# Attention and two MLPs on one core: the softmax quotient and a share of the squares go from VectorE to ScalarE

## The chip, the cores and the metric

One Trainium2 chip, one of its cores. The metric is device time in microseconds (us), the median of several runs. The engines of the core work side by side, each through its own list of instructions in order: TensorE (PE in the rows, PEld its weight loads), VectorE (DVE), ScalarE (ACT), GpSimd (POOL) and SyncE (SP), whose queue here issues every DMA. TensorE writes into PSUM, in banks; GpSimd works on SBUF only.

## What is computed

The reference has three parts, in fp32. Attention over 2 batches, 8 heads, 768 tokens of 64 dimensions, with a mask from hash buckets:

```python
mask = q_bucket[:, :, :, None] == k_bucket[:, :, None, :]
scores = np.where(mask, scale * np.matmul(q, k.transpose(0, 1, 3, 2)), -1000000000.0)
attn = np.exp(scores - np.max(scores, axis=-1, keepdims=True))
attn = attn / (np.sum(attn, axis=-1, keepdims=True) + 1e-09)
x = np.matmul(attn, v)                       # then heads side by side: 1536 tokens x 512
```

Then two MLPs one after the other, 512 to 2048 to 512, each with weights of its own:

```python
r = np.maximum(x @ w_in, 0.0);  x = (r * r) @ w_out      # layer 0
h = x @ w_in;  out = np.maximum(0.01 * h, h) @ w_out     # layer 1
```

The inputs q, k, v, proj and the weights of both layers are float32 or wider, and the weights are unpacked on the chip from pairs of 32-bit words.

## The kernel before

**Slots.** Attention runs over 48 slots a batch: 4 pairs of heads, 2 heads, 6 tiles of 128 queries. A slot is: TensorE's scores (line 659, four matmuls), VectorE's row maximum (lines 679 and 683), ScalarE's exponential (line 688), and the transposition of the result p as two fp16 halves. The high half is a cast (lines 717 and 718), the low half a subtraction, on GpSimd (line 721) or VectorE (line 722). In batch 0 half of the slots go through TensorE for the transposition (lines 699, 707, 710), all others through a DMA (line 735). After that TensorE multiplies p with v (lines 756 to 758, 18 matmuls a slot, written into the PSUM tile `av`). `av` has two halves of three slots each. When three slots are summed, `finish` works out the quotient: on VectorE, `rd` = sum times scale (line 780), its reciprocal (line 784) and the product with the 3 x 64 columns (line 785) into `xtok`. A half of `av` can be written again after that.

Every 12 slots a new pair of heads is prepared (`prep`): sizes (line 441), scales over the partitions (`level`, lines 398 to 419), fp16 halves (lines 479, 492, 501), hash bits (lines 546, 558, 564), v (lines 608, 614).

**Banks for scores.** Batch 0 has three banks for scores, `s` and the two of `sx`. When the MLP begins, `sx` becomes the four banks `acc` of the MLP, so that batch 1 has the one bank `s`: the scores of a slot can be written when the maximum of the slot ahead has been read.

**MLP.** The weights of layer 0 are fetched, unpacked on VectorE (lines 883, 887, 890), split into a high part (lines 927, 928) and a low one (line 932), and written back for a second use. A unit of TensorE is 12 matmuls (lines 938 to 940). After an "up" unit of layer 0, ScalarE takes the Relu (line 977, `rt`), VectorE multiplies by it (line 980, `gx`), and the result is split again (lines 990 and 995). After a "down" unit the result is copied or added (lines 1059 and 1061). Four groups of 8 up and 8 down units make one batch of a layer.

**The stages.** Batch 0's attention comes first. Its results are transposed (line 802) and split (lines 811 and 812). Then layer 0 of batch 0 runs on TensorE between the slots of batch 1's attention. From 400 us on there is MLP alone: layer 0 of batch 1, then layer 1 of both.

**What sets the order.** Every step is given to `Plan` by `do(due, reads, writes, engine=(cost, function))`, with what it reads and writes, a due time, and a cost of its own for each engine that may do it; the first engine named is the one it prefers. `order` plays the steps through with these costs and places each on an engine at a time; the instructions are then written in that order, and stay in it on the chip. The constants at the head of the function (`DONE_AT`, `PITCH1` and the rest) shift due times.

Of the kernel before, what the change touches and what calls it, by code (L numbers as in the profile page):

```python
# [14 lines left out]
ACTF = mybir.ActivationFunctionType  # L15
ALU = mybir.AluOpType
# [158 lines left out]
def lsh_attention_moe_moe_kernel(  # L175
# [17 lines left out]
    nc = tc.nc  # L193
    B, H, S, D = q.shape
# [22 lines left out]
    SINGLE = 5  # L217
    BEHIND = 4
    BY_PE = 2
    PE_LAG = 3.65  # L220
    SECOND = -1.46
    VLATE = -5.42
    OWN = 0.30
    MARGIN = 0.99
    MAX_AT = 2.01
    EXP_AT = -0.44
    HI_AT = 7.80
    LO_AT = -14.89
    TURN_AT = -1.33
    DONE_AT = -8.87  # L230
    PREP_AT = -1.03
    PREP_STEP = 0.35
    LAG0 = -6.35
    FETCH = 13.02
    CONVERT = 16.38
    KEEP = -12.32
    AGAIN = 45.39
    FETCH0 = 3.26
    LEAD0 = 57.48
    CONVERT0 = -9.27  # L240
    LOAD1_AT = -14.58
    HALVE = 19.67
    T_UP = 16384.0
    SIZE16 = 6.00
    const = ctx.enter_context(tc.tile_pool(name="const", bufs=1))
# [518 lines left out]
    def finished(b, i, d):  # L764

        pr, n = divmod(i, SLOTS)
        h = n // NTB
        _, x3 = held[b, pr]
        half, x = i // HB % 2, i % HB
        summed.add((b, i))  # L770
        first = i - x
        if any((b, y) not in summed for y in range(first, first + HB)):
            return False
        tq = first % NTB + HB - 1
        rd = rd_[half]
        hh = 2 * pr + h

        def finish():
            acc = psum["av"][0][:, half]
            nc.vector.tensor_scalar(  # L780
                out=rd, in0=acc[:, :, D:D + 1], scalar1=SUM_EPS, scalar2=sc[x3][:, 2:3],
                op0=ALU.add, op1=ALU.mult,
            )
            nc.vector.reciprocal(out=rd, in_=rd)
            nc.vector.tensor_tensor(
                out=xtok[:, tq - HB + 1:tq + 1, hh * D:(hh + 1) * D], in0=acc[:, :, 0:D],
                in1=rd.to_broadcast([128, HB, D]), op=ALU.mult,
            )

        do(  # L790
            d + DONE_AT, [("av", half, y) for y in range(HB)] + [("sc", x3)], [("x", hh, tq // HB), ("rd", half)],
            dve=(0.75, finish),
        )
        return True

# [161 lines left out]
    def up(b, L, f, j, d):  # L957

        r = f % FG
        key, extra, bank = acc_bank()  # L960
        def part(c):
            w = w16(r) if L else (wi[:, r, 0, :], wi[:, r, 1, :])
            xs = [(x16(b, j, s) if L else xt[b, j, s])[:, c, :] for s in "hl"]
            three(bank()[:, :HALF], [y[:, c * 128:(c + 1) * 128] for y in w], xs, c == 0, c == NC - 1)

        us = (G1_T, G1_T16)[L]
        for c in range(NC):
            do(
                d, [("w16", r, y) if L else ("w", "i", r, y) for y in range(2)]
                + [("x16" if L else "xt", b, j, y, c) for y in "hl"],  # L970
                [key] + (extra if c == 0 else []), pe=(us / NC, lambda c=c: part(c)),
            )
        rt, gx = rt_[ring("rt", 2)], gx_[ring("gx", 2)]
        rk, gk = ("rt", turns["rt"] % 2), ("gx", turns["gx"] % 2)
        d += G1_T
        if L == 0:
            do(d, [key], [rk], act=(0.37, lambda: nc.scalar.activation(
                out=rt, in_=bank()[:, :HALF], func=ACTF.Relu
            )))
            do(d + 0.4, [key, rk], [gk], dve=(0.47, lambda: nc.vector.scalar_tensor_tensor(  # L980
                out=gx, in0=bank()[:, :HALF], scalar=0.0, in1=rt, op0=ALU.max, op1=ALU.mult
            )))
        else:
            do(d, [key, ("back", b)], [rk], act=(0.37, lambda: nc.scalar.activation(  # L984
                out=rt, in_=bank()[:, :HALF], func=ACTF.Copy, scale=back[b][:, 0:1]
            )))
            do(d + 0.4, [key, rk, ("back", b)], [gk], dve=(0.47, lambda: nc.vector.scalar_tensor_tensor(  # L987
                out=gx, in0=bank()[:, :HALF], scalar=back[b][:, 1:2], in1=rt, op0=ALU.mult, op1=ALU.max
            )))
        do(d + 1.1, [gk, "given"], [("g", r, j, 0)], act=(0.42, lambda: nc.scalar.copy(out=g_of(r, j)[0], in_=gx)),  # L990
           dve=(Port(0.27), lambda: nc.vector.tensor_copy(out=g_of(r, j)[0], in_=gx)))

        def low(eng):
            gh, gl = g_of(r, j)
            eng.tensor_tensor(out=gl, in0=gx, in1=gh.bitcast(FP32), op=ALU.subtract)  # L995

        do(d + 1.6, [gk] + [("g", r, j, 0)], [("g", r, j, 1)],
           pool=(0.98, lambda: low(nc.gpsimd)), dve=(Port(0.47), lambda: low(nc.vector)))
# [108 lines left out]
        return d  # L1107


    PITCH = 1.88  # L1110
    LEAD = 8.07
    START = 11.59
    MLP_OFF = 10.91
# [155 lines left out]
```

## Time and profile before

| | |
|---|---|
| median of 3 runs | 803.62 us (801.91 to 806.05) |
| the profiled execution, its own time | 803.74 us |
| its span, first to last instruction | 802.0 us |
| TensorE busy | 721.7 us (90%) |
| VectorE busy | 578.0 us (72%) |
| ScalarE busy | 433.3 us (54%) |
| GpSimd busy | 325.5 us (41%) |
| mean granted TensorE clock | 0.957 |
| chain of work that ended last | PE 75%, DVE 19%, issue 3%, ACT 2%, DMA 1% |

A busy share over the whole span mixes three stages with different limits. The table of busy time by stretch splits them: a stretch in which TensorE is busy throughout at a granted clock of 1.00 can be shortened only by giving it less to do, and in the others the question is what TensorE waits for. "Granted clock" is TensorE's clock as a share of 2.4 GHz; its lower level is 1.2 GHz.

### The profile page before, as it was taken

Reading aid. Unit: us, or ns where it says so; the run is one execution under the profiler, and the core shown is the slowest. Engines: PE = TensorE matmul, PEld = TensorE weight load, DVE = VectorE, ACT = ScalarE, POOL = GpSimd, SP = SyncE. Lnnn points to the kernel's source line nnn. Section 1 sums busy time; section 2 is a strip of 40 time slices with the busy share of each in tenths; the row PEclk is TensorE's granted clock in tenths of the full one; section 3 lists DMA queues with packets and bytes.
Section 4 is the critical chain, followed back from the end, with each engine's and each line's share of the span. In section 5 each row is a group of like instructions: output and inputs, shape, how many; then the busy total and the mean of one; then the engine's idle time right before and its main releaser. Section 6 shows DMA issues by size and latency. Waiting matters only on the chain.

```text
span 802.0 us, 14410 instructions
## 1 busy us (share of the span) xinstructions
PE 721.7 (90%) x5526; PEld 591.9 (74%) x5526; DVE 578.0 (72%) x1170; ACT 433.3 (54%) x739; POOL 325.5 (41%) x258
## 2 busy tenths in 40 slices
PE   3686767689999796899999999999999999999998
PEld 2474545477998684798899999996776766767766
DVE  6899999968998999989655544768547539638422
ACT  5877787647757577457555513456454044153330
POOL 2324233325565456558643614327025033232320
PEclk9899989869999997799999999999999999999999
DMA  3496777697998999998731324123303302210112
GB/s 118 78 219 108 189 149 207 120 236 139 222 264 165 185 248 227 197 270 179 163 77 50 94 64 132 30 76 105 105 1 106 105 1 87 81 44 27 40 40 78
DMA packets 185860, 100.81 MB, mean 126 GB/s; under 512 B 149440, under 2 KB 171968, under 8 KB 185792
## 3 DMA queue, kind: packets, MB, share of 16 engines
q1 hardware_dynamic: 185792, 99.90, 51.9%
q8 instruction: 43, 0.70, 0.4%
q14 instruction: 25, 0.20, 0.1%
HBM read 51.38 MB, written 11.53 MB: 78 GB/s over the span
## 4 chain that ended last, share of the span: by engine, by line
PE 75%; DVE 19%; issue 3%; ACT 2%; DMA 1%; POOL 0%; SPq 0%; DVEq 0%; ACTq 0%; POOLq 0%
PE acc L938 21%; PE acc L939 21%; PE acc L940 21%; PE s L659 4%; DVE ep L679 3%; PE av L756 2%; PE av L758 2%; PE av L757 1%; DVE s L492 1%; PE sx L699 1%; DVE lo L679 1%; DVE sm L683 1%; DVE pt L679 1%; DVE lg L679 1%; PE sx L659 1%
## 5 line engine op out<-in xcount | busy, mean ns | idle before, releaser
L995 POOL TENSOR_TENSOR g<-gx,g 128x384 fp32r<-128x384 f32 x113 | 124.5, 1115 | 164.6 <-ACT g L990 150.4
L721 POOL TENSOR_TENSOR ep<-ep 128x768 f16<-128x768 f32 x44 | 77.9, 1777 | 79.2 <-ACT ep L717 50.6
L932 POOL TENSOR_TENSOR wo<-w,wo 128x512 fp32r<-128x512 f32 x37 | 53.5, 1457 | 121.9 <-ACT wo L927 78.5
L938 PE MATMUL acc<-xh,wi 128*128 128x384 f32 x256 | 91.4, 357 | 1.2 <-DVE gx L980 1.0
L938 PE MATMUL acc<-g,wo 128*128 128x384 f32 x256 | 88.9, 347 | 1.8 <-DVE part L1061 1.3
L939 PE MATMUL acc<-xl,wi 128*128 128x384 f32 x256 | 87.7, 343 | 0.0
L940 PE MATMUL acc<-xh,wi 128*128 128x384 f32 x256 | 87.7, 343 | 0.0
L688 ACT ACTIVATE ep<-ep,sm,scs 128x768 f32<-128x768 f32 x60 | 61.6, 1027 | 47.5 <-DVE sm L683 46.2
L984 ACT ACTIVATE rt<-acc,rawq 128x384 f32<-128x384 f32 x64 | 37.1, 579 | 91.4 <-PE acc L940 91.3
L939 PE MATMUL acc<-g,wo 128*128 128x384 f32 x256 | 85.8, 335 | 0.0
L940 PE MATMUL acc<-g,wo 128*128 128x384 f32 x256 | 85.8, 335 | 0.0
L659 PE MATMUL s<-t 128*128 128x384 f16 x288 | 66.2, 358 | 19.4 <-DVE sm L683 17.3
L987 DVE SCALAR_TENSOR_TENSOR gx<-acc,rawq,rt 128x384 f32<-128x384 f32 x64 | 39.0, 614 | 58.1 <-ACT rt L984 55.4
L938 PE MATMUL acc<-wo,g 128*128 128x512 f32 x192 | 76.6, 399 | 0.0
L1061 DVE TENSOR_TENSOR part<-acc,part 128x384 f32<-128x384 f32 (+1 forms) x66 | 38.9, 591 | 51.3 <-PE acc L940 51.0
L659 PEld LDWEIGHTS <-t 128*128 128x128 f16 x384 | 36.6, 105 | 52.8 <-issue 41.1
L940 PE MATMUL acc<-wo,g 128*128 128x512 f32 x192 | 74.8, 390 | 0.0
L939 PE MATMUL acc<-wo,g 128*128 128x512 f32 x192 | 74.7, 389 | 0.0
L990 ACT CAST g<-gx 128x384 fp32r<-128x384 f32 x123 | 61.6, 508 | 19.2 <-DVE gx L987 11.0
L890 DVE SCALAR_TENSOR_TENSOR w<-wide,w 128x512 int32<-128x512 int32 x64 | 53.2, 839 | 0.4
L679 DVE TENSOR_SCALAR_CACHE_REDUCE ep<-s 128x768 f32<-128x768 f32 x48 | 45.6, 950 | 10.7 <-PE s L659 9.1
L887 DVE SCALAR_TENSOR_TENSOR w<-wide,w 128x512 int32<-128x512 int32 x64 | 52.8, 830 | 0.4
(202 smaller groups left out, 2006.3 us busy)
## 6 DMA issues: line engine op xcount, KB each, us to landing
wide<-in_moe_w_in_dram SPq DMA_DIRECT2D x32, 512.0 KB, 4.8
w<-w SPq DMA_DIRECT2D x64, 256.0 KB, 3.4
wide<-in_moe_w_out_dram SPq DMA_DIRECT2D x32, 512.0 KB, 4.7
rawq<-in_q_dram SPq DMA_DIRECT2D x8, 384.0 KB, 3.5
rawk<-in_k_dram SPq DMA_DIRECT2D x8, 384.0 KB, 3.8
rawv<-in_v_dram SPq DMA_DIRECT2D x8, 384.0 KB, 4.0
out_dram<-part SPq DMA_DIRECT2D x6, 256.0 KB, 2.0
out_dram<-ep SPq DMA_DIRECT2D x6, 256.0 KB, 2.0
```

The lines of the kernel that those rows point to most:

```text
L659: nc.tensor.matmul(out=ps[:, j, :HALF], lhsT=t[x][:, 0, n, :], rhs=t[x][:, 1, h * NTB + j * HB:h * NTB + (j + 1) * HB, :].rearrange("p n c ...
L679: nc.vector.tensor_scalar(out=e.rearrange("p (a c) -> p a c", a=2), in0=s_tile(r)[:, :, :HALF], scalar1=FLOOR, scalar2=None, op0=ALU.max, ...
L688: do(d + EXP_AT, [smk, ("scs", x3)] + early, ek, act=(0.96, lambda: nc.scalar.activation(out=e, in_=e, func=ACTF.Exp, scale=scs[x3][:, 0:1 ...
L721: pool=(1.65, lambda: nc.gpsimd.tensor_tensor(out=p[:, 1, :], in0=e, in1=p[:, 0, :], op=ALU.subtract)),
L887: (Port(0.6), lambda: nc.vector.scalar_tensor_tensor(out=oi, in0=t[:, :, 0], scalar=29, in1=oi, op0=ALU.logical_shift_right, op1=ALU.bitwi ...
L890: (Port(0.6), lambda: nc.vector.scalar_tensor_tensor(out=oi, in0=t[:, :, 1], scalar=-0x40000000, in1=oi, op0=ALU.bitwise_and, op1=ALU.bitw ...
L932: eng.tensor_tensor(out=lo, in0=o, in1=hi.bitcast(FP32), op=ALU.subtract)
L938: nc.tensor.matmul(out=acc, lhsT=st[0], rhs=mv[0], start=first, stop=False)
L939: nc.tensor.matmul(out=acc, lhsT=st[0], rhs=mv[1], start=False, stop=False)
L940: nc.tensor.matmul(out=acc, lhsT=st[1], rhs=mv[0], start=False, stop=last)
L990: do(d + 1.1, [gk, "given"], [("g", r, j, 0)], act=(0.42, lambda: nc.scalar.copy(out=g_of(r, j)[0], in_=gx)), dve=(Port(0.27), lambda: nc. ...
L995: eng.tensor_tensor(out=gl, in0=gx, in1=gh.bitcast(FP32), op=ALU.subtract)
```

## The change

Two steps of the kernel get another engine, and the constants of the planner other values.

The quotient is two steps now. `divisor` stays on VectorE (the former lines 780 and 784). The product with `rd` prefers ScalarE, as three activations with a scale for each partition (128 x 64 each), with VectorE's one instruction as the second choice. The square of layer 0 may be done on ScalarE from `rt`, without PSUM; in batch 0 every second f (8 of 16, each for two halves of the tokens) has ScalarE alone, the other steps prefer VectorE and may go to ScalarE.

```diff
-    PE_LAG = 3.65
+    PE_LAG = 4.14
...
+    FIN_ACT = 1
+    SQ_ACT = 2
...
-    CONVERT = 16.38
+    CONVERT = 10.99
...
-        def finish():
+        def divisor():
             acc = psum["av"][0][:, half]
...
             nc.vector.reciprocal(out=rd, in_=rd)
+
+        def to():
+            return xtok[:, tq - HB + 1:tq + 1, hh * D:(hh + 1) * D]
+
+        def divide():
             nc.vector.tensor_tensor(
-                out=xtok[:, tq - HB + 1:tq + 1, hh * D:(hh + 1) * D], in0=acc[:, :, 0:D],
-                in1=rd.to_broadcast([128, HB, D]), op=ALU.mult,
-            )
-
+                out=to(), in0=psum["av"][0][:, half, :, 0:D], in1=rd.to_broadcast([128, HB, D]), op=ALU.mult
+            )
+
+        def divide_act():
+            for y in range(HB):
+                nc.scalar.activation(
+                    out=to()[:, y, :], in_=psum["av"][0][:, half, y, 0:D], func=ACTF.Copy, scale=rd[:, y, :]
+                )
+
+        av = [("av", half, y) for y in range(HB)]
+        scale = ("sc", x3)
+        do(d + DONE_AT, av + [scale], [("rd", half)], dve=(0.46, divisor))
         do(
-            d + DONE_AT, [("av", half, y) for y in range(HB)] + [("sc", x3)], [("x", hh, tq // HB), ("rd", half)],
-            dve=(0.75, finish),
+            d + DONE_AT + 0.5, av + [("rd", half)], [("x", hh, tq // HB)],
+            **({"act": (0.6, divide_act), "dve": (0.28, divide)} if FIN_ACT else
+               {"dve": (0.28, divide), "act": (0.6, divide_act)})
         )
...
-            do(d + 0.4, [key, rk], [gk], dve=(0.47, lambda: nc.vector.scalar_tensor_tensor(
-                out=gx, in0=bank()[:, :HALF], scalar=0.0, in1=rt, op0=ALU.max, op1=ALU.mult
-            )))
+            ways = dict(
+                dve=(0.47, lambda: nc.vector.scalar_tensor_tensor(
+                    out=gx, in0=bank()[:, :HALF], scalar=0.0, in1=rt, op0=ALU.max, op1=ALU.mult
+                )),
+                act=(0.39, lambda: nc.scalar.activation(out=gx, in_=rt, func=ACTF.Square)),
+            )
+            if b == 0 and f % SQ_ACT == SQ_ACT - 1:
+                ways = {"act": ways["act"]}
+            do(d + 0.4, [key, rk], [gk], **ways)
...
-    PITCH1 = 3.98
-    PREP1_AT = -8.21
+    PITCH1 = 4.50
+    PREP1_AT = -11.08
```

The matmuls, the DMAs and their number stay as they are. With the planner's new values the whole order moves on every engine. By the new order 31 of the 32 quotients and 33 of the 64 squares stand on ScalarE, and GpSimd has 68 low halves of p where it had 63 (VectorE 4 where it had 9). The lines of the new kernel lie 2 to 22 behind those of the old one: its 681, 685, 690, 719, 782, 786, 899, 903 and 906 are the former 679, 683, 688, 717, 780, 784, 883, 887 and 890, and 798 is the new activation.

VectorE in batch 1's attention, from slot 75 to slot 78 of the 96 (`ep,s` is a row maximum, `sm` its scaled value, `w` and `wide` are weights that are unpacked, `s_78` the halves of q and k of the next pair). Before:

```order
L679 TENSOR_SCALAR ep,s_146<-s_146 128x768
L683 TENSOR_SCALAR sm_98<-s_146,scs_93 128x1
L417 TENSOR_TENSOR pw_89<-t_142,floors 128x3
L418 RECIPROCAL am_87<-pw_89 128x3
L419 TENSOR_TENSOR sc_91<-am_87,targets 128x3
L887 SCALAR_TENSOR_TENSOR w_119<-wide_115,w_119 128x512
L679 TENSOR_SCALAR ep,s_146<-s_146 128x768
L683 TENSOR_SCALAR sm_99<-s_146,scs_93 128x1
L492 SCALAR_TENSOR_TENSOR s_78<-rawq,sc_91,s_78 128x12x64
L492 SCALAR_TENSOR_TENSOR s_78<-rawk,sc_91,s_78 128x12x64
L679 TENSOR_SCALAR ep,s_146<-s_146 128x768
L683 TENSOR_SCALAR sm_100<-s_146,scs_93 128x1
```

Now, slots 72 to 74, where the scores follow each other without a unit of the MLP between them:

```order
L681 TENSOR_SCALAR ep,s_146<-s_146 128x768
L685 TENSOR_SCALAR sm_98<-s_146,scs_93 128x1
L782 TENSOR_SCALAR rd_102<-av_150,sc_92 128x3
L786 RECIPROCAL rd_102<-rd_102 128x3
L720 CAST ep<-ep 128x768
L899 TENSOR_SCALAR w_118<-wide_114 128x512
L906 SCALAR_TENSOR_TENSOR w_117<-wide_113,w_117 128x512
L681 TENSOR_SCALAR ep,s_146<-s_146 128x768
L685 TENSOR_SCALAR sm_99<-s_146,scs_93 128x1
L903 SCALAR_TENSOR_TENSOR w_118<-wide_114,w_118 128x512
L899 TENSOR_SCALAR w_119<-wide_115 128x512
L681 TENSOR_SCALAR ep,s_146<-s_146 128x768
```

The halves of the next pair stand behind slot 77 now, where units of the MLP lie between the scores, and the quotient's product is gone from this list.

ScalarE at the end of batch 0's attention in the new order (`xtok` with `av` and `rd` is the quotient, `lg` and `lo` are tiles of p):

```order
L798 ACTIVATE xtok<-av_150,rd_102 128x64 x3
L690 ACTIVATE lg<-lg,sm_101,scs_93 128x768
L709 CAST lo<-sx_154 128x768
L690 ACTIVATE lo<-lo,sm_100,scs_93 128x768
L798 ACTIVATE xtok<-av_150,rd_103 128x64 x3
L719 CAST pt<-lo 128x768
L481 ACTIVATE s_78<-rawq,sc_91 128x12x64
L610 ACTIVATE vv_84<-rawv,sc_91 128x12x64
L798 ACTIVATE xtok<-av_150,rd_102 128x64 x3
```

Each of these groups of three waits for VectorE's `rd` at its place in the list, and the exponentials and casts behind it wait with it.

## Rows read from the trace of the kernel before

**Rows 1.** Busy time by stretch of the span; the first line names the columns.

```profile
core 0: us, PE busy (x) PEld busy (x) DVE busy (x) ACT busy (x) POOL busy (x), PEclk, DMA share, GB/s
0.00:160.00 160.00, 106.83 (x1377) 79.85 (x1378) 144.70 (x362) 118.95 (x161) 52.48 (x49) 0.91 0.66 148
160.00:180.00 20.00, 16.79 (x136) 14.36 (x135) 13.58 (x31) 9.95 (x18) 5.06 (x4) 0.69 0.93 241
180.00:260.00 80.00, 77.38 (x661) 69.98 (x660) 71.92 (x138) 55.03 (x89) 48.16 (x32) 0.98 0.92 195
260.00:280.00 20.00, 14.89 (x161) 12.32 (x160) 18.14 (x43) 10.52 (x14) 8.19 (x5) 0.91 0.98 190
280.00:300.00 20.00, 19.75 (x188) 17.98 (x185) 19.39 (x36) 15.25 (x25) 11.35 (x9) 1.00 1.08 245
300.00:330.00 30.00, 20.11 (x209) 14.17 (x206) 28.47 (x64) 20.34 (x29) 18.01 (x13) 0.72 1.06 228
330.00:400.00 70.00, 68.88 (x620) 63.07 (x618) 56.85 (x114) 41.56 (x62) 46.37 (x31) 1.00 0.90 200
400.00:800.00 400.00, 397.10 (x2194) 320.18 (x2193) 225.00 (x389) 161.71 (x344) 135.90 (x119) 1.00 0.21 67
```

**Rows 2.** TensorE's waits from 178 to 402 us: us in total, times, longest.

```profile
PE s L659 <- DVE sm L683: 6.7, 7, 3.3
PE av L756 <- DVE xtok L785: 3.6, 3, 3.1
PE av L756 <- DMA pt<-ep: 3.4, 3, 1.8
```

**Rows 3.** VectorE in order of time: start us, us, then the instruction.

```profile
296.50 0.94 DVE L722 TENSOR_TENSOR ep<-ep 128x768 f16<-128x768 f32 x1
297.36 0.94 DVE L679 TENSOR_SCALAR_CACHE_REDUCE ep<-s 128x768 f32<-128x768 f32 x1
298.24 0.13 DVE L679 DVE_READ_ACCUMULATOR ep<-s 128x1 f32 x1
298.41 0.22 DVE L683 TENSOR_SCALAR sm<-s,scs 128x1 f32<-128x1 f32 x1
298.55 0.42 DVE L883 TENSOR_SCALAR w<-wide 128x512 int32<-128x512 int32 x1
...
306.30 2.02 DVE L722 TENSOR_TENSOR ep<-ep 128x768 f16<-128x768 f32 x1
```

**Rows 4.** TensorE in order of time: a slot's 18 sums begin, then its scores.

```profile
303.23 0.20 PE L756 MATMUL av<-vv,pt 128*128 128x65 f16 x1
...
303.80 0.49 PE L659 MATMUL s<-t 128*128 128x384 f16 x2
```

**Rows 5.** The chain that ended last, one slot's scores: start us, us, what.

```profile
300.14 0.65 PE s L659 x4
```

**Rows 6.** Groups of instructions over the span: count, busy us, mean ns, idle before.

```profile
L785 DVE TENSOR_TENSOR xtok<-av,rd 128x192 f32<-128x192 f32 x32 | 11.4, 357 | 1.1
L980 DVE SCALAR_TENSOR_TENSOR gx<-acc,rt 128x384 f32<-128x384 f32 x64 | 34.4, 550 | 19.5 <-ACT rt L977 19.5
L722 DVE TENSOR_TENSOR ep<-ep 128x768 f16<-128x768 f32 x9 | 13.3, 1484 | 0.0
L721 POOL TENSOR_TENSOR ep<-ep 128x768 f16<-128x768 f32 x44 | 77.9, 1777 | 79.2 <-ACT ep L717 50.6 <-DVE ldiag L407 13.6 <-DVE s L492 5.6
L977 ACT ACTIVATE rt<-acc 128x384 f32<-128x384 f32 x64 | 30.9, 488 | 39.5 <-PE acc L940 39.3
L479 ACT ACTIVATE s<-rawq,sc 128x768 f16<-128x768 f32 x7 | 6.5, 928 | 0.8 <-DVE sc L419 0.8
L479 ACT ACTIVATE s<-rawq,sc 128x384 f16<-128x384 f32 x1 | 0.6, 615 | 2.5 <-DVE sc L419 2.5
```

**Rows 7.** TensorE's waits for the quotient, 0 to 180 us.

```profile
PE s L802 <- DVE xtok L785: 2.1, 1, 2.1
PE av L756 <- DVE xtok L785: 1.9, 3, 1.1
```

More of the change, by code (lines that the diff above doesn't have):

```diff
@@ L219, in lsh_attention_moe_moe_kernel @@
     BY_PE = 2
-    PE_LAG = 3.65
-    SECOND = -1.46
-    VLATE = -5.42
+    PE_LAG = 4.14
+    SECOND = -3.30
+    VLATE = -5.27
     OWN = 0.30
+    FIN_ACT = 1
+    SQ_ACT = 2
     MARGIN = 0.99
[L225 to L229, printed above, removed]
+    MAX_AT = 2.19
+    EXP_AT = 0.39
+    HI_AT = 2.36
+    LO_AT = -4.03
+    TURN_AT = -1.95
     DONE_AT = -8.87
     PREP_AT = -1.03
-    PREP_STEP = 0.35
-    LAG0 = -6.35
-    FETCH = 13.02
-    CONVERT = 16.38
[L236 to L242, printed above, removed]
+    PREP_STEP = 0.42
+    LAG0 = -4.16
+    FETCH = 13.37
+    CONVERT = 10.99
+    KEEP = -12.16
+    AGAIN = 21.71
+    FETCH0 = 3.54
+    LEAD0 = 58.07
+    CONVERT0 = -4.11
+    LOAD1_AT = -17.77
+    HALVE = 19.44
     T_UP = 16384.0
@@ L976, in up @@
         if L == 0:
-            do(d, [key], [rk], act=(0.37, lambda: nc.scalar.activation(
+            do(d, [key], [rk], act=(0.39, lambda: nc.scalar.activation(
                 out=rt, in_=bank()[:, :HALF], func=ACTF.Relu
             )))
-            do(d + 0.4, [key, rk], [gk], dve=(0.47, lambda: nc.vector.scalar_tensor_tensor(
-                out=gx, in0=bank()[:, :HALF], scalar=0.0, in1=rt, op0=ALU.max, op1=ALU.mult
-            )))
+            ways = dict(
[7 more added lines that the diff above has]
+            do(d + 0.4, [key, rk], [gk], **ways)
         else:
@@ L1107, in group @@
         return d
[L1110 to L1113, printed above, removed]
+    PITCH = 1.89
+    LEAD = 9.06
+    START = 11.43
+    MLP_OFF = 10.00
     MLP_AT = START + N_ATT * PITCH + MLP_OFF
     STRETCH = 1.87
-    AT1_OFF = -0.41
+    AT1_OFF = -2.35
     AT1 = MLP_AT + AT1_OFF
-    PITCH1 = 3.98
-    PREP1_AT = -8.21
-    PREP1_STEP = 6.95
+    PITCH1 = 4.50
+    PREP1_AT = -11.08
+    PREP1_STEP = 6.71
     COLD = 1.05
```

## The prediction

> **What bounds the kernel now.** I read the busy time by stretch first, since it separates the stages [rows 1]. From 400 us on TensorE is busy 397.1 of 400 us at a granted clock of 1.00. Nothing is to be had there from other engines, and its matmuls stay the same, so those 400 us and the last 2 us of the span stay. Up to 160 us VectorE bounds: 144.7 of 160 us busy, TensorE 106.8, ScalarE 119.0. From 180 to 400 us, where batch 1's attention runs between units of the MLP, TensorE should be busy throughout, and is not: it idles 80 - 77.4 = 2.6, 20 - 14.9 = 5.1, 0.3, 30 - 20.1 = 9.9 and 70 - 68.9 = 1.1 us in the five stretches, 19.0 us in all. A granted clock below 1.00 costs it more: 0.02 x 80 + 0.09 x 20 + 0.28 x 30 = 11.8 us. Together **30.8 us are lost** between 180 and 400, of them 6.9 us (5.1 + 1.8) at 260 to 280 and 18.3 us (9.9 + 8.4) at 300 to 330, where the clock of 0.72 is a mix of the two levels, 1.2 and 2.4 GHz. VectorE is busy 28.5 of 30 us there: it has a backlog. The waits agree [rows 2]: 6.7 us for the row maximum, 3.6 for the quotient, only 3.4 for a DMA.
>
> Why there: with the one bank `s`, the scores of a slot wait for the maximum of the slot ahead. In the order there are runs of slots with no unit of the MLP between the scores. I call each such pair of slots a dense step. In a dense step TensorE has 0.65 us of scores [rows 5] and 0.57 us of sums (303.23 to 303.80) [rows 4], 1.2 us. VectorE has at least the maximum, from 297.36 to 298.55, 1.2 us [rows 3], and whatever else stands in its list.
>
> **The change, part by part.** Prices are spacings: a row on VectorE or ScalarE begins some 0.09 us before the one ahead of it ends (298.41 + 0.22 against 298.55) [rows 3], so I take 0.09 off a duration.
>
> *The quotient.* VectorE loses 0.357 - 0.09 = 0.27 us each, 31 times: 8.4 us [rows 6]. On ScalarE, with a scale by partition, 768 columns take 0.928 us and 384 take 0.615, so a column costs 0.81 ns and 64 columns 0.615 - 320 x 0.00081 = 0.36 us, in spacings 0.27, three of them 0.8 us. That is no such row in the trace but a line through two; bounds are 3 x 0.2 (the slope with a smaller start) and 3 x 0.53 (the 384-wide row itself), and I take 0.8, since it has the same kind of operands. A group so costs ScalarE 0.5 us more than it saves VectorE. The Trainium skill, "ScalarE: Activation LUTs", Rules for kernel authors, says to do plain products on VectorE and not on ScalarE; taken alone, 31 groups would come to 31 x 0.5 = 16 us lost, which is the side of the last rival below. ScalarE is busy 119.0 of 160 us and 142.7 of 220 where VectorE is busy 144.7 and 194.8 [rows 1], so I charge the difference only where TensorE waits for a quotient.
>
> *The squares.* VectorE loses 0.550 - 0.09 = 0.46 us each; between the first and the last slot of batch 1 the order has 4 of them where it had 30, so 26 x 0.46 = 12.0 us. ScalarE gains 26 x 0.4 (the Relu's 0.488 less 0.09) = 10.4 us there.
>
> *What else the order moves.* Four low halves of p fewer on VectorE there, 4 x 1.4 = 5.6 us (1.484 - 0.09), and 14 quotients, 3.9 us. With smaller moves of weight preparation VectorE's rows between the first and last maximum of batch 1, each at its median spacing, come to 154 us where they came to 182. ScalarE's rows rise by some 20 to 23 us on 143 of 220.
>
> *Stage 1, 0 to 180 us.* VectorE loses 15 quotients, 4.1 us. But the order puts more unpacking of weights ahead of the turn: by row spacings VectorE's list up to batch 1's first maximum is only 1.0 us shorter. ScalarE gets 15 x 0.8 = 12 us more, 131 of 160, which it has room for. The quotient now takes 0.5 us longer and waits for a place in ScalarE's list; TensorE waited for it four times, 2.1 + 1.9 us [rows 7]. Four times 0.5 is +2.0. Sum **+1.0 us**; bounds -3 (the row sum and two waits that vanish) and +8 (0.5 us at all 16 groups).
>
> *Stage 2, 180 to 400 us.* The dense steps are counted from the order, and their price is VectorE's rows in them less TensorE's. Before there were two runs, of 3 and of 6 steps. VectorE's rows in them come to 12.0 and 22.4 us, TensorE's to 4.3 and 7.9: 22.2 us lost by rows, against 25.2 us measured in the two stretches, a factor of 1.14. That the sum lands so near is my reason to use it. Now the runs are of 4 steps (slots 72 to 76, VectorE 10.9, TensorE 4.9), 3 steps (88 to 91, 7.0 and 3.6) and two single steps (3.6 and 1.7; 2.8 and 1.2): 6.0 + 3.4 + 1.9 + 1.6 = 12.9 us, times 1.14 is 14.6. There are nine dense steps before and now; what is gone is the work of VectorE in them, above all the halves of the next pair, the low halves of p and the quotients. The other 5.6 us I leave. Gain 25.2 - 14.6 = **-10.6 us**. Bounds: 3 us, if the shorter runs still take the clock down and rows lengthen, and 30.8 - 12.9 = 17.9 us, if the factor is 1 and the rest goes too. Outside the runs VectorE now has slack: at no slot after the first few does its row sum run ahead of TensorE's, where it was up to 18 us ahead, and by the same sums the unpacking of a group's weights ended up to 15 us late, and now ends 8 us early or more.
>
> *The turn at 400 us.* One unit more lies behind the last slots as cover for the transpositions: -0.5. The squares of batch 1 after 400 us lie under TensorE's matmuls; ScalarE, busy 162 of 400, hides them, and if it did not, a unit would wait at most some 0.4 us each.
>
> **Sum.** 803.74 + 1.0 - 10.6 - 0.5 = 793.6, against the profiled execution's own time (span 802.0 and 1.7 around it); it lies 0.1 over the median of 803.62. I forecast **793.5 us**.
>
> **The rivals.**
> - *The backlog goes whole, and the clock stays up.* Runs of 4 and 3 steps are shorter than that of 6, and the run of 3 kept a clock of 0.91. Then stage 2 gains 17.9 and stage 1 breaks even: 803.7 - 17.9 - 0.5 = 785. Against it: any dense step still has TensorE idle.
> - *The price belongs to the step, not to VectorE's rows.* Nine steps before at 25.2 / 9 = 2.8 us and nine now: no gain in stage 2, 803.7 + 1.0 - 0.5 - 1 (four units come earlier) = 803. Against it: the rows explain the difference between the two runs.
> - *GpSimd lengthens VectorE's rows.* The same subtraction on VectorE took 0.94 us and 2.02 us [rows 3]. Five more of 1.78 us on GpSimd [rows 6] may each lengthen a row by 1.08, 5.4 us in all if it hits dense steps: 799. The Trainium skill, "SBUF — State Buffer", SBUF: two separate sides, has the two engines take a shared pair of ports in turn for a whole instruction; by that rule, the spread of those two rows agrees.
> - *Slower: ScalarE's list waits.* A quotient at its place in ScalarE's list waits for VectorE's `rd`, which waits for TensorE's sums, and the exponentials behind it wait too; the next scores of batch 0 hang on these. If each of 15 groups costs stage 1 a full 1.0 us, 15 us come against 10.6 + 0.5: 803.7 + 15 - 11 = 808. It ends slower from 0.75 us a group on. Against it: three banks of scores and a ScalarE idle a quarter of the time.
>
> That the planner would leave the steps on VectorE is out: the order shows them moved.
>
> **Chances.** The forecast 0.47, the first rival 0.20, the second 0.15, the third 0.08, the fourth 0.10. A measurement here can tell about 0.5% from no change, so the band is 799.6 to 807.6. Faster: 0.46 of the forecast, 0.20, 0.04 and 0.04, 0.74. Same: 0.01 + 0.10 + 0.03 + 0.02 = 0.16. Slower: 0.10, nearly all from the last. The range 782 to 803 takes in the forecast, the first rival and half of the second.
>
> **What would show it.** In the profile after, VectorE's busy time should be 30 us down and ScalarE's 30 to 35 up. TensorE's waits between the start of the MLP and the end of batch 1's attention should fall from 19 to some 12 us, in three or four places instead of two, with a granted clock of 0.97 or more over the stage where it was 0.95. The turn to batch 1 should lie at 180 us as before, give or take 4, and the last stage should take 402 us again. I am wrong if that turn comes after 185 us (the quotient on ScalarE is dear), if the dense steps still take 2.8 us each, or if TensorE waits in a place that this text does not name, such as for a weight or a DMA.

## The result and the profile after

The changed kernel takes 797.76 us (median, 796.27 to 800.61) beside 805.88 us for the kernel before: a ratio of 0.9918 with a 95% interval of 0.9901 to 0.9936. Beside the experiments it was run again: 799.28 us against 802.84, a ratio of 0.9959 (0.9937 to 0.9981). So the change is faster, by 3.6 to 8.1 us, and I can't say closer than that. The forecast was 793.5.

The profiled execution of the changed kernel took 800.61 us (span 798.8), at the upper end of its runs; the second one took 799.38 (span 797.5). Both stand against 803.74 of the kernel before.

Busy time by stretch, as in [rows 1]:

```profile
core 0: us, PE busy (x) PEld busy (x) DVE busy (x) ACT busy (x) POOL busy (x), PEclk, DMA share, GB/s
0.00:160.00 160.00, 106.50 (x1385) 78.95 (x1386) 141.03 (x354) 126.06 (x201) 52.89 (x49) 0.93 0.68 153
160.00:180.00 20.00, 17.52 (x148) 15.62 (x146) 12.11 (x34) 12.44 (x25) 4.54 (x4) 0.78 0.78 207
180.00:260.00 80.00, 78.35 (x694) 71.46 (x693) 69.50 (x125) 64.51 (x115) 52.59 (x35) 1.00 0.98 213
260.00:280.00 20.00, 18.86 (x186) 16.54 (x185) 17.01 (x35) 14.97 (x30) 13.07 (x9) 1.00 1.10 191
280.00:300.00 20.00, 14.15 (x128) 11.37 (x126) 18.44 (x27) 13.61 (x26) 17.14 (x12) 0.79 1.01 230
300.00:330.00 30.00, 25.54 (x241) 21.37 (x242) 23.45 (x54) 20.39 (x30) 15.56 (x10) 0.80 0.95 208
330.00:400.00 70.00, 61.25 (x581) 54.97 (x578) 55.86 (x100) 47.73 (x86) 45.07 (x31) 0.95 0.92 194
400.00:798.00 398.00, 394.67 (x2186) 318.47 (x2182) 222.08 (x383) 163.18 (x353) 132.81 (x117) 1.00 0.21 68
```

Read the PE column from 180 to 400 us against [rows 1]: the idle time has moved, from 260 to 280 and 300 to 330 to 280 to 300, 300 to 330 and 330 to 400, and has not shrunk (19.0 us before, 21.9 now). The clock's loss is 4.2 + 6.0 + 3.5 = 13.7 us where it was 11.8. TensorE's waits from 178 to 402 us have another name at their head than in [rows 2], and a sum no smaller, 21.7 us against 19.9; the first three of six are:

```profile
PE av L758 <- DVE rd L782: 12.4, 4, 3.5
PE s L661 <- DVE sm L685: 4.8, 6, 1.2
PE av L758 <- DMA pt<-ep: 2.2, 2, 1.5
```

Landmarks tell where the microseconds lie: the start of the maximum's second instruction (`sm`) of batch 1's first slot, 48, and of its last slot, 95, and the starts of the MLP's 961st and 2871st matmul. In us, between landmarks:

| profiled execution of | start to slot 48 | slot 48 to 95 | 95 to matmul 961 | 961 to 2871 |
|---|---|---|---|---|
| before | 180.3 | 216.8 | 43.0 | 355.6 |
| after | 179.1 | 216.2 | 41.4 | 355.5 |
| after, second | 177.9 | 216.1 | 41.4 | 355.6 |
| forecast change | +1.0 | -10.6 | -0.5 | 0 |

**The stage that was to give 10.6 us gave 0.6 or 0.7.** What is won lies at its two ends.

### The profile page after: what moved, and what is told of

It reads as the page before. It is cut to its first block, busy times and chain, and to the rows that moved or that the text cites. A ratio compares the mean times of both kernels' runs of the same rounds, so it can differ in the third digit from the quotient of the medians.

```text
span 798.8 us, 14492 instructions
## 1 busy us (share of the span) xinstructions
PE 716.8 (90%) x5526; PEld 588.8 (74%) x5526; DVE 559.5 (70%) x1106; ACT 462.9 (58%) x860; POOL 333.7 (42%) x263
## 4 chain that ended last, share of the span: by engine, by line
PE 60%; DVE 7%; issue 2%; ACT 2%; POOL 0%; DVEq 0%; ACTq 0%; POOLq 0%
PE acc L954 19%; PE acc L955 18%; PE acc L956 18%; DVE ep L681 2%; PE s L661 2%; DVE w L903 1%; DVE w L906 1%; DVE w L899 1%; PE av L758 1%; PE av L760 1%; PE av L759 1%; ACT ep L719 0%; ACT ep L690 0%; DVE sm L685 0%; DVE part L1083 0%
## 5 line engine op out<-in xcount | busy, mean ns | idle before, releaser
L1017 POOL TENSOR_TENSOR g<-gx,g 128x384 fp32r<-128x384 f32 x115 | 126.2, 1110 | 149.4 <-ACT g L1012 142.0
L723 POOL TENSOR_TENSOR ep<-ep 128x768 f16<-128x768 f32 x49 | 88.5, 1809 | 79.6 <-ACT ep L719 55.7
L948 POOL TENSOR_TENSOR wo<-w,wo 128x512 fp32r<-128x512 f32 x34 | 47.6, 1408 | 123.6 <-ACT wo L943 64.3
L954 PE MATMUL acc<-xh,wi 128*128 128x384 f32 x256 | 90.0, 351 | 0.3 <-DVE part L1083 0.3
L956 PE MATMUL acc<-xh,wi 128*128 128x384 f32 x256 | 86.4, 338 | 0.0
L903 DVE SCALAR_TENSOR_TENSOR w<-wide,w 128x512 int32<-128x512 int32 x64 | 58.6, 921 | 0.4
L906 DVE SCALAR_TENSOR_TENSOR w<-wide,w 128x512 int32<-128x512 int32 x64 | 57.6, 906 | 0.6
```

What stands on the lines that cost most here:

```text
L723: pool=(1.65, lambda: nc.gpsimd.tensor_tensor(out=p[:, 1, :], in0=e, in1=p[:, 0, :], op=ALU.subtract)),
L903: (Port(0.6), lambda: nc.vector.scalar_tensor_tensor(out=oi, in0=t[:, :, 0], scalar=29, in1=oi, op0=ALU.logical_shift_right, op1=ALU.bitwi ...
L906: (Port(0.6), lambda: nc.vector.scalar_tensor_tensor(out=oi, in0=t[:, :, 1], scalar=-0x40000000, in1=oi, op0=ALU.bitwise_and, op1=ALU.bitw ...
L948: eng.tensor_tensor(out=lo, in0=o, in1=hi.bitcast(FP32), op=ALU.subtract)
L954: nc.tensor.matmul(out=acc, lhsT=st[0], rhs=mv[0], start=first, stop=False)
L956: nc.tensor.matmul(out=acc, lhsT=st[1], rhs=mv[0], start=False, stop=last)
```

## Experiments

Each group of runs had the kernel before beside it (802.94, 802.84 and 804.28 us); ratios are to that.

**The moves and the order, apart.** The first three kernels keep the changed kernel's order, and with it five more low halves on GpSimd, and hand the moved work back to VectorE, at its places: the quotients, the squares, both. Here `undo` is true for the step kinds named.

```
-            plan.steps[n][2][e][1]()
+            ways = plan.steps[n][2]
+            undo = e == "act" and plan.kinds.get(n) in ('quotient', 'square')
+            (plan.squares.get(n) or ways["dve"] if undo else ways[e])[1]()
```

> The changed kernel with its own order kept; only the 31 products with the reciprocal are written out on VectorE again, at the places where ScalarE had them. Theory A (VectorE's rows in the dense steps are the price, as forecast): VectorE gets 31 x 0.27 = 8.4 us back, about half of it where it binds, so 801 to 803 against 797.8 of the changed kernel and 805.9 of the one before (ratio to before 0.995 to 0.997). Theory B (the new order alone made the gain): no change from 0.992. Theory C (the product on ScalarE holds up the next sums, since both halves of av are one tile): the product ends sooner on VectorE, so faster than the changed kernel, 0.987 to 0.990.

> The changed kernel with its own order kept; only the 33 squares are written out on VectorE again. Theory A: VectorE gets 33 x 0.46 = 15 us back, 12 of them in batch 1's attention, and the dense steps lengthen: 802 to 805, ratio to before 0.995 to 0.999. Theory B: 0.992 as the changed kernel. Theory C says nothing of the squares: 0.992 to 0.995.

> The changed kernel with its own order kept, and both the products and the squares written out on VectorE: only the new order and the five low halves on GpSimd are left of the change. Theory A: VectorE's 24 us are back and so is its backlog, 804 to 808, ratio to before 0.998 to 1.003. Theory B: 0.992, the moves did nothing. A ratio between says how much each has.

Measured: 803.89 us, 1.0011 (0.9997 to 1.0024); 807.59, 1.0062 (1.0043 to 1.0082); 812.41, 1.0113 (1.0091 to 1.0134). All three lie above the range that theory A gave them; theories B and C, by which nothing or a gain was to come, fall.

The fourth does the reverse: before's order and constants, with the products and the odd blocks' squares of batch 0 on ScalarE at the places where VectorE had them.

```
             nc.vector.reciprocal(out=rd, in_=rd)
-            nc.vector.tensor_tensor(
...
+            for y in range(HB):
+                nc.scalar.activation(
+                    out=xtok[...], in_=acc[:, y, 0:D], func=ACTF.Copy, scale=rd[:, y, :]
+                )
...
+            if b == 0 and f % 2:
+                do(..., nc.scalar.activation(out=gx, in_=rt, func=ACTF.Square))
```

> The kernel before with its own order, its own constants and its own places; only the engine of 32 products and 32 squares (odd blocks of batch 0's first layer) is now ScalarE. Theory A (what counts is the work taken off VectorE): at least half of the gain is here, 0.994 to 0.997 of before (798 to 800.5). Theory B (work moved without a new order finds no room, since ScalarE's list waits at places chosen for VectorE): 1.000 to 1.008. The product forms are those of the changed kernel, 0.31 us each.

> The changed kernel itself, on the same chip as the variants, against a before of 802.9. If the gain belongs to the kernel and not to one execution: 0.990 to 0.994 of before (795 to 798), and a second profile whose stage from 180 to 400 us loses less than the 35.5 us (21.9 idle, 13.7 clock) of the first, since the first profiled execution was the slowest of its nine. If the first profile is typical, the loss in that stage is again 33 to 37 us and the gain sits elsewhere, a little in each stage.

Measured: moves alone 811.11 us, 1.0117 (1.0080 to 1.0155); the changed kernel 0.9959. This makes a square of four:

| | work on VectorE | work on ScalarE |
|---|---|---|
| order of before | 1 | 1.0117 |
| order of after | 1.0113 | 0.9959, 0.9918 |

**Either half alone costs about 1%; only together they gain.** The moves alone land on theory B's side, beyond its 1.008; that the order alone makes the gain falls with the second row. Where they lose is in the landmarks, in us:

| profiled execution of | start to slot 48 | slot 48 to 95 | 95 to matmul 961 | 961 to 2871 |
|---|---|---|---|---|
| moves alone | 186.5 | 223.4 | 41.2 | 355.6 |
| order alone, both handed back | 182.7 | 223.0 | 42.5 | 357.1 |
| products handed back | 179.6 | 216.2 | 42.0 | 357.1 |
| squares handed back | 175.9 | 224.2 | 41.9 | 357.1 |

From slot 48 to 95 the squares handed back cost 8.0 us against the changed kernel, the products nothing. The last stage is 1.5 us longer in all three hand-back kernels, whatever they hand back: one row of GpSimd (`g`) takes 6.30 us there where it takes 1.24 in the changed kernel, and TensorE waits for it. So 0.2% of each of these three times is not the price of the moved work; why that row is long stays open.

With the moves alone, ScalarE waits at its quotients. The groups of the quotient's rows on ScalarE up to 400 us, first of the kernel with the moves alone, then of the changed one (count, busy us, mean ns, idle before):

```profile
L786 ACT ACTIVATE xtok<-av,rd 128x64 f32<-128x64 f32 x87 | 21.0, 313 | 31.1 <-DVE rd L784 29.8 <-DVE pw L417 1.3
```

```profile
L798 ACT ACTIVATE xtok<-av,rd 128x64 f32<-128x64 f32 x90 | 21.3, 312 | 11.1 <-DVE rd L786 8.0 <-PE av L760 3.1
```

31.1 us of waiting before 87 rows is the fourth rival at work: a quotient placed where VectorE had it waits for `rd`, with the exponentials queued behind it. The first stage pays 6.2 us for it. The new order has the quotient later in ScalarE's list, and 11.1 us are left.

With the order alone it is the squares. ScalarE's casts of the activations (`g`) wait for VectorE's square, from 182 to 407 us, in the kernel with both handed back:

```profile
ACT ep L692 <- DVE sm L687: 32.2, 28, 3.5
ACT g L1019 <- DVE gx L1000: 13.3, 11, 2.5
```

That wait was 4.5 us in four places in the kernel before, and there is none in the changed one. TensorE's own waits in the same window name VectorE's rows and not `g`: 27.2 us in all, 14.9 of them for `rd` and 7.3 for the maximum, where the changed kernel has 21.7, 12.4 and 4.8. That `g`'s wait is what costs TensorE its time is not shown.

**The dense steps.** The next two kernels go at the wait that now leads, that of sums for a divisor (`rd`, L782) that reads the triple ahead of them: one such sum begins at 292.81 us, behind an L782 from 292.55 to 292.76. Both halves of `av` are one tile in one bank, so the sum waits for the quotient of the *other* half, too, and the planner doesn't know it. The first kernel tells the planner and lets it order anew. The second (`acc3`) takes the dependency away: three banks instead of four for the MLP's units, and the free bank for batch 1's second half of `av`.

```
+        other = [("av", 1 - half, y) for y in range(HB)]
-        do(d + DONE_AT, av + [scale], [("rd", half)], dve=(0.46, divisor))
+        do(d + DONE_AT, av + [scale] + other, [("rd", half)], dve=(0.46, divisor))
...
-            d + DONE_AT + 0.5, av + [("rd", half)], [("x", hh, tq // HB)],
+            d + DONE_AT + 0.5, av + [("rd", half)] + other, [("x", hh, tq // HB)],
```

> The changed kernel, whose planner is told that the quotient's two steps also read the other half of av, which is how the instructions wait on the chip (both halves are one tile); the order is planned anew with the same constants. Theory C: TensorE's waits of 12.4 us for the divisor in batch 1's attention fall below 5 and the time to 790 to 794 (ratio to before 0.980 to 0.986). Theories A and B: those waits stand for VectorE's backlog or for the dense step itself, so that they turn up as waits for the row maximum, and the time stays at 796 to 800 (0.988 to 0.994).

```
+    def av_of(b, half):
+        return psum["av2"][0] if b and half else psum["av"][0][:, half]
...
-                open_pool("acc", [128, 512], 4)
+                open_pool("acc", [128, 512], 3)
+                open_pool("av2", [128, HB, D + 1])
```

> The changed kernel with three banks for the MLP's units instead of four, and the free bank given to the second triple of batch 1's sums, so that no sum waits for the quotient of the triple ahead of it in the other half of the same tile (12.4 of 22 us waited by TensorE in 178 to 402 us were at such sums, all in the runs of dense steps). The order is replanned for three banks. If these waits are a price of their own: 4 to 10 us less than the changed kernel, 0.980 to 0.987 of before. If VectorE's rows set the pace of a dense step and the wait only names the last of them: the same waits come at the scores (maximum) instead, and the time is that of the changed kernel within 0.4%. If three banks are too few for the units: slower, above 1.000.

Measured: told 806.46 us, 1.0042 (1.0027 to 1.0057), slower than either expectation has it; the waits for `rd` are gone from its trace and 10.1 us of waits for the products on ScalarE stand there. Its order is new on every engine, so it doesn't decide between the two. Three banks 800.13 us, 0.9971 (0.9948 to 0.9993), which is the changed kernel's 799.28 within 0.1%. The first two waits of the kernel with three banks, from 178 to 402 us:

```profile
PE s L661 <- DVE sm L685: 15.5, 7, 4.5
PE av L761 <- DMA pt<-ep: 3.0, 2, 1.6
```

The wait for `rd` is gone and has come back at the scores, 15.5 us where it was 4.8. Both are waits for the same list of VectorE. Its order is new as well, so a part stays open: from slot 48 to 95 it takes 212.7 us, 3.4 less than the changed kernel, and up to slot 48 181.4, 3.5 more.

**VectorE's rows, and what GpSimd does to them.** Here is VectorE in the changed kernel's longest run of dense steps:

```profile
288.36 1.69 DVE L899 TENSOR_SCALAR w<-wide 128x512 int32<-128x512 int32 x1
290.08 1.36 DVE L903 SCALAR_TENSOR_TENSOR w<-wide,w 128x512 int32<-128x512 int32 x1
291.37 0.94 DVE L681 TENSOR_SCALAR_CACHE_REDUCE ep<-s 128x768 f32<-128x768 f32 x1
...
293.54 0.42 DVE L899 TENSOR_SCALAR w<-wide 128x512 int32<-128x512 int32 x1
293.88 2.13 DVE L906 SCALAR_TENSOR_TENSOR w<-wide,w 128x512 int32<-128x512 int32 x1
295.94 0.94 DVE L681 TENSOR_SCALAR_CACHE_REDUCE ep<-s 128x768 f32<-128x768 f32 x1
...
300.57 0.68 DVE L906 SCALAR_TENSOR_TENSOR w<-wide,w 128x512 int32<-128x512 int32 x1
301.17 2.13 DVE L903 SCALAR_TENSOR_TENSOR w<-wide,w 128x512 int32<-128x512 int32 x1
```

and GpSimd at that time:

```profile
288.12 1.65 POOL L723 TENSOR_TENSOR ep<-ep 128x768 f16<-128x768 f32 x1
289.72 2.58 POOL L1017 TENSOR_TENSOR g<-gx,g 128x384 fp32r<-128x384 f32 x2
293.76 3.75 POOL L723 TENSOR_TENSOR ep<-ep 128x768 f16<-128x768 f32 x2 [1.47 <-ACT ep L690]
...
301.11 1.65 POOL L723 TENSOR_TENSOR ep<-ep 128x768 f16<-128x768 f32 x1 [1.93 <-ACT ep L719]
```

The same row takes 0.42 or 1.69, 0.68 or 2.13 us, and the long ones lie beside a row of GpSimd. To price it, two kernels cut GpSimd's subtractions to 64 columns from the second use of a place on, in the changed kernel and in the kernel before, each in its own order. They leave out most low halves. The edit for the weights stands here for all three kinds.

```
-            eng.tensor_tensor(out=lo, in0=o, in1=hi.bitcast(FP32), op=ALU.subtract)
+            n = few(("w", kind, r), DM) if eng is nc.gpsimd else DM
+            eng.tensor_tensor(out=lo[:, :n], in0=o[:, :n], in1=hi[:, :n].bitcast(FP32), op=ALU.subtract)
```

> The changed kernel in its own order, but GpSimd's subtractions (low halves of p, of the weights and of the activations) write only 64 columns from the second use of a place on; the output is not the reference's. If GpSimd's rows lengthen VectorE's (L903 and L906 921 and 906 ns against 830 and 839 before; single rows 2.1 us): these rows fall to a mean of about 0.65 us, VectorE's busy time falls by 15 to 35 us, and the time by 4 to 12 us against the changed kernel (785 to 793). If the two engines do not disturb each other: the rows keep their means and the time stays within 0.3%, since GpSimd is not on the path.

> The kernel before, its order untouched, with GpSimd's subtractions cut to 64 columns from the second use of a place on (output not the reference's), as in gp_few. It asks how much of VectorE's time GpSimd takes in the kernel before. In the changed kernel the same cut gave 9.6 us (799.28 to 789.66). Theory C (the change's gain is eaten because GpSimd lengthens VectorE's rows more than it did): the cut gives clearly less here, 2 to 6 us, so 797 to 801 (0.992 to 0.998), and the distance between the two kernels without GpSimd's load is the forecast one, 8 to 11 us. Theory D (the price belongs to the dense step and GpSimd's load is the same in both): the cut gives 8 to 11 us here too, 0.987 to 0.990, and the two kernels stay 3 to 4 us apart.

Measured: 789.66 us, 0.9845 (0.9814 to 0.9876), and 793.68 us, 0.9875 (0.9841 to 0.9910). The cut is worth 9.6 us in the changed kernel, whose VectorE is busy 70 us less by it (558.1 to 488.1, twice what was expected at most), and 10.6 in the kernel before: by the whole times, theory D of the last expectation and not its theory C.

By stages it is not so even. Between the landmarks the kernel before takes 177.5, 214.5, 40.5 and 355.6 us with the cut, the changed kernel 176.0, 208.5, 41.4 and 355.5. From slot 48 to 95 the cut so gives 2.3 us before and 7.6 after, and without GpSimd's load the change gains 6.0 us where it gains 0.6 or 0.7 with it: in this stage, theory C's side. This is one execution each, and that of the kernel before took 796.14 us, the longest of its six; if all it has over their median lay in this stage, 3.5 of the 6.0 us would be left. The cut also has GpSimd's own results ready sooner, and no run separates that from VectorE's shorter rows.

VectorE's groups that unpack weights, from 180 to 400 us, before, after, and after with the cut (count, busy us, mean ns), for the last two with the maximum and the MLP's additions beside them:

```profile
L890 DVE SCALAR_TENSOR_TENSOR w<-wide,w 128x512 int32<-128x512 int32 x24 | 22.7, 949 | 0.1
L887 DVE SCALAR_TENSOR_TENSOR w<-wide,w 128x512 int32<-128x512 int32 x24 | 20.0, 834 | 0.2
L883 DVE TENSOR_SCALAR w<-wide 128x512 int32<-128x512 int32 x24 | 13.8, 584 | 0.1
```

```profile
L903 DVE SCALAR_TENSOR_TENSOR w<-wide,w 128x512 int32<-128x512 int32 x24 | 27.5, 1151 | 0.1
L906 DVE SCALAR_TENSOR_TENSOR w<-wide,w 128x512 int32<-128x512 int32 x24 | 27.0, 1128 | 0.2
L899 DVE TENSOR_SCALAR w<-wide 128x512 int32<-128x512 int32 x24 | 21.9, 916 | 0.0
L681 DVE TENSOR_SCALAR_CACHE_REDUCE ep<-s 128x768 f32<-128x768 f32 x47 | 44.7, 951 | 19.4 <-PE s L661 12.1 <-issue 2.4 <-PE t L414 2.1
L1083 DVE TENSOR_TENSOR part<-acc,part 128x384 f32<-128x384 f32 x24 | 12.8, 548 | 6.6 <-PE acc L956 6.6
```

```profile
L914 DVE SCALAR_TENSOR_TENSOR w<-wide,w 128x512 int32<-128x512 int32 x24 | 17.1, 716 | 0.1
L917 DVE SCALAR_TENSOR_TENSOR w<-wide,w 128x512 int32<-128x512 int32 x24 | 16.4, 687 | 0.2
L910 DVE TENSOR_SCALAR w<-wide 128x512 int32<-128x512 int32 x24 | 11.1, 468 | 3.3 <-DMA w<-w 3.3
L688 DVE TENSOR_SCALAR_CACHE_REDUCE ep<-s 128x768 f32<-128x768 f32 x46 | 43.9, 955 | 35.7 <-PE s L668 23.5 <-issue 5.9 <-PE t L421 3.4
L1098 DVE TENSOR_TENSOR part<-acc,part 128x384 f32<-128x384 f32 x24 | 13.0, 550 | 7.1 <-PE acc L969 7.1
```

The same 72 rows take 56.5 us before, 76.4 after (74.4 in the second execution) and 44.6 where GpSimd does little. With the cut in the kernel before they take 42.7, one row lying outside the window:

```profile
L901 DVE SCALAR_TENSOR_TENSOR w<-wide,w 128x512 int32<-128x512 int32 x24 | 16.9, 706 | 0.1
L898 DVE SCALAR_TENSOR_TENSOR w<-wide,w 128x512 int32<-128x512 int32 x24 | 16.4, 684 | 0.2
L894 DVE TENSOR_SCALAR w<-wide 128x512 int32<-128x512 int32 x23 | 9.4, 417 | 0.4 <-DMA wide<-in_moe_w_in_dram 0.4
```

So GpSimd's load lengthens them by 13.8 us before and by 31.8 after. They take 54.9 us with the moves alone and 67.1 with the order alone: the new order by itself brings half of what they gained in length, and the moves the other half, but only in that order. The maximum and the additions, which read PSUM, keep their duration with the cut and without.

**The DMA engines.** Their share is 0.92 to 1.10 from 180 to 400 us. Two kernels fetch an eighth of the raw weights' columns from the second use of a buffer on (and so compute with stale weights), alone and with GpSimd's cut.

```
+                n = 16 if ("wide", y) in fetched else 128
...
-                    nc.sync.dma_start(out=t.rearrange("p d w -> p (d w)"), in_=src[f * 128:(f + 1) * 128, :])
+                    nc.sync.dma_start(
+                        out=t.rearrange("p d w -> p (d w)")[:, :8 * n], in_=src[f * 128:(f + 1) * 128, :8 * n]
+                    )
```

> The changed kernel in its own order, but from the second use of a buffer on a fetch of raw weights brings an eighth of the columns (64 KB for 512); the output is not the reference's. The DMA engines' share is 0.90 to 1.11 from 180 to 400 us. If they are what holds the dense steps up: the waits on transposed p (3.4 us) and the pace of the weights go, 5 us or more less than the changed kernel (under 0.990 of before). If VectorE's rows hold them: within 2 us of the changed kernel (0.993 to 0.998), since VectorE is busy 1.97 of every 2 us from 286 to 306.

> Both cuts, GpSimd's and the weight fetches (output not the reference's). In gp_few VectorE no longer fills the dense steps; there TensorE waits 3.96 us for a transposed p and VectorE 3.03 us for a DMA of weights. If the DMA engines are next in line: 3 to 6 us less than gp_few (783 to 787, 0.976 to 0.981 of before) and those two waits gone. If not: within 1.5 us of gp_few's 0.9845.

Measured: 797.61 us, 0.9931 (0.9903 to 0.9960), between the two results of the changed kernel; with both cuts 785.28 us, 0.9772 (0.9737 to 0.9807), 0.7% below GpSimd's cut alone. The fetch cut alone took the share from 0.98 to 0.78 between 180 and 260 us and from 1.01 to 0.77 between 280 and 300. VectorE is busy 18.9 and 19.5 of the 20 us from 286 to 306 in the changed kernel's two executions, a little less than the first expectation has it. So no price of the transfers is shown while VectorE's rows are long, and they come next when these are short. In the run of dense steps with GpSimd's cut TensorE waits (280 to 305 us):

```profile
PE av L769 <- DMA pt<-ep: 4.0, 1, 4.0
PE av L769 <- DVE rd L793: 2.4, 2, 1.7
```

and with both cuts the first of these is 1.8 us.

**Twice the dose.** One constant puts every square of batch 0 on ScalarE, in an order planned anew.

```
-    SQ_ACT = 2
+    SQ_ACT = 1
```

> The changed kernel with all 64 squares of the first batch on ScalarE instead of every second block of them (SQ_ACT = 1), replanned: twice the dose of one half of the change, correct output. Some 30 more rows of 0.55 us leave VectorE, most between 180 and 400 us. If every row taken off VectorE there shortens the stage: 4 to 8 us less than the changed kernel (0.986 to 0.991 of before). If the rows that leave are ones GpSimd never lengthens (their input lies in PSUM) and those that stay are lengthened in their place, or ScalarE's list gets late: no gain or a loss, 0.995 to 1.005.

Measured: 796.92 us, 0.9920 (0.9892 to 0.9948). That interval takes in both results of the changed kernel, so no gain is shown, and no loss. No kernel with the whole computation beat the changed one beyond its interval.

## Why the prediction was right, and where it was wrong

The sign and the range were right. The size was not: 10.2 us were forecast, 3.6 to 8.1 measured, and the working was wrong where most of it lay. That the time still fell into the range is in part luck, since what was won came before and behind the stage that was to give it. Two of the signs named failed as well: in that stage TensorE idles 21.9 us, not some 12, and its granted clock is 0.94 (1 - 13.7 / 220), not 0.97.

**The dense steps: the failed term.** The step that failed is "times 1.14 is 14.6 ... Gain 25.2 - 14.6 = -10.6 us". A dense step is the time from the start of one slot's scores to the next, with no unit between. In the changed kernel's run of four and in the same run with both moves handed back:

```profile
288.49 0.81 PE L661 MATMUL s<-t 128*128 128x384 f16 x4
...
293.77 1.47 PE L661 MATMUL s<-t 128*128 128x384 f16 x4
...
297.25 1.44 PE L661 MATMUL s<-t 128*128 128x384 f16 x4 [1.03 <-DVE sm L685]
...
301.16 1.47 PE L661 MATMUL s<-t 128*128 128x384 f16 x4
...
307.48 0.83 PE L661 MATMUL s<-t 128*128 128x384 f16 x2
```

```profile
296.21 0.81 PE L663 MATMUL s<-t 128*128 128x384 f16 x4
301.39 1.47 PE L663 MATMUL s<-t 128*128 128x384 f16 x4
304.87 1.44 PE L663 MATMUL s<-t 128*128 128x384 f16 x4 [1.03 <-DVE sm L687]
308.58 1.47 PE L663 MATMUL s<-t 128*128 128x384 f16 x4
315.10 1.15 PE L663 MATMUL s<-t 128*128 128x384 f16 x3
```

The four steps take 18.99 and 18.89 us. All nine of a kernel:

| kernel | runs of dense steps, us | nine steps |
|---|---|---|
| before | 9.85 (3), 23.85 (6) | 33.7 |
| after | 18.99 (4), 10.35 (3), 2.28, 2.78 | 34.4 |
| after, second | 17.92, 10.85, 2.28, 2.78 | 33.8 |
| after's order, both moves handed back | 18.89, 9.49, 2.86, 3.04 | 34.3 |
| before, GpSimd's cut | 9.65, 22.64 | 32.3 |
| after, GpSimd's cut | 16.17, 8.54, 2.28, 2.78 | 29.8 |
| after, both cuts | 13.40, 8.43, 2.27, 2.78 | 26.9 |

The 2.78 and the 3.04 hold three matmuls of a unit; without that step eight steps of the changed kernel take 31.6 us. Nine steps cost the same with the moves and without. The second rival's forecast (no gain in this stage, 0.15) so came true, but its reason, "the price belongs to the step, not to VectorE's rows", did not: with GpSimd's cut the nine steps fall to 29.8 us in the changed kernel and to 32.3 in the one before. The text had named the sign: "I am wrong if ... the dense steps still take 2.8 us each". They nearly do; by this measure TensorE loses (34.4 - 11.4) / 9 = 2.6 us a step, and lost (33.7 - 12.2) / 9 = 2.4.

Two things went wrong in the reckoning. The first is the price of the rows. I summed VectorE's list in the run of four at median spacings and had 10.9 us. VectorE works from 288.36 to 306.08 us there without a gap, 17.7 us. Nine rows of unpacking take 12.5 of them; at 0.42 and 0.68 us they would take 5.3. A median from the whole stage is not the price in a stretch where GpSimd is busy 17.1 of 20 us. That the factor of 1.14 fitted two runs of before was no proof of the model. The second is where the work stands that leaves VectorE. A square belongs to a unit and a dense step has none, so of the 30 squares between slots 48 and 95 of the kernel before only two lie in dense steps, the one here and one at 325.15 us, and in the run with both handed back one:

```profile
304.02 0.55 DVE L980 SCALAR_TENSOR_TENSOR gx<-acc,rt 128x384 f32<-128x384 f32 x1
```

```profile
296.50 0.56 DVE L1000 SCALAR_TENSOR_TENSOR gx<-acc,rt 128x384 f32<-128x384 f32 x1 [0.39 <-ACT rt L996]
```

The forecast looked for the gain in the dense steps and left what lies outside them ("The other 5.6 us I leave"); there, in the new order, the squares are worth 8.0 us.

What makes a dense step 3 us long with both cuts, I have not settled. VectorE's rows are a part, transfers another, and the 2.78 and 2.28 us of the single steps move with neither.

**GpSimd lengthens VectorE's rows: right, and three to four times the size.** The third rival had 5.4 us for it in all. In 180 to 400 us VectorE was to lose 28 us of rows and lost 194.8 - 184.3 = 10.5; the 72 unpacking rows alone are 19.9 us longer. That is enough to explain why VectorE's busy time fell by 18.5 us over the span (to 559.5) and not by 30. Over the whole time the cut gives the two kernels the same within the intervals. But between slots 48 and 95 it gives 7.6 us after and 2.3 before, so about 5 of the 10 us that are missing there (3, if the longer execution is allowed for) go with GpSimd's load. What took the rest stays open. The Trainium skill, "SBUF — State Buffer", SBUF: two separate sides, says that VectorE has to wait for the ports that it shares with GpSimd only in a row that reads two inputs from SBUF or runs in a mode with two ports. The trace agrees: the maximum takes 951 ns with GpSimd's load and 955 without, while the unpacking goes from 1151 to 716. The squares and the products read PSUM too, and in the kernel before they keep their duration with the load and without, 546 and 550 ns, 357 and 357 (up to 402 us); so VectorE was safe from GpSimd while it did them. Whether taking them away drives GpSimd's load onto the other rows stays open: in the new order it goes with more lengthening (67.1 to 76.4 us), in the old one with none (56.5 to 54.9).

**Stage 1: +1.0 forecast, -1.2 and -2.4 measured.** The wait that was priced is there, and larger: TensorE's waits for the quotient rose from 4.0 us [rows 7] to 8.9, 5.4 of them of `av` at four places. The turn came at 179.1 us, inside 180 give or take 4. What made up for the wait is not shown: with the products on ScalarE the new order reaches slot 48 at 179.1, 177.9 and (squares handed back) 175.9 us, with the products on VectorE at 179.6 and 182.7, so single executions scatter by some 3 us. The fourth rival's danger was real: in the old order the same move costs this stage 6.2 us. What disarmed it is the new place of the quotient, as the 31.1 and 11.1 us above say; the prediction read it from the order without giving it a number.

**The price of a product on ScalarE** was sized well: 0.312 us a row and three in 0.72, against 0.36 and 0.8 through the line of [rows 6]. **The turn at 400 us** gave 1.6 where 0.5 was forecast. The last stage takes the same time, as forecast. ScalarE's busy time rose by 29.6 us, a shade under the 30 to 35.

**Where the gain came from.** Not from shorter dense steps. Against the same order without the moves (start to slot 48, 48 to 95, 95 to matmul 961) the second execution is 4.8, 6.9 and 1.1 us shorter, with equal dense steps: 34.3 and 33.8. So in the middle stage it lies in the steps with units, and it is the squares: handed back alone they take that stage to 224.2 us, the products alone leave it at 216.2. With the squares back TensorE waits there for VectorE's `rd`, maximum and `part` 22.3 us, where it waited 17.5. The new order gave most of that away again against the kernel before; both together leave 4 to 8 us.

## What to carry over

Work moved to another engine needs the order that goes with it: measure all four corners, since here each half alone was about 1% slower and together they were 0.4 to 0.8% faster. Before counting a row that leaves an engine as a gain, look whether it stands in the stretch that waits at all; here the dense steps held two of 30 squares. And price SBUF rows of VectorE from the stretch in question, by what GpSimd does there, not from a median over the stage.

## What the hardware showed that I had not expected

- Two rows of VectorE between SBUF operands, 512 columns of int32 and one behind the other, took 0.68 and 2.13 us by what GpSimd did. Cutting GpSimd from 143 to 42 us of work between 180 and 400 us took 76.4 - 44.6 = 31.8 us off 72 rows of unpacking, and nothing off rows that read one operand from PSUM (`part<-acc,part`, 548 and 550 ns).
- A dependency can be wider than the data. Sums into one half of a PSUM tile waited for the read of the other half to end; four such waits made 12.4 us. With the halves in two tiles and two banks (which of the two counts is not separated) the wait moved to the next row in line, and the whole time stayed as it was.
- A cut of the fetched weights from 512 to 64 KB showed no gain alone (0.9931) and 0.7% behind GpSimd's cut: what looked saturated (a share of about 1.0 for 200 us) was not seen to bind until another bound had gone.
